# Attention followed by a feed-forward block on one core: another set of ranks for a scheduler that orders the program

## The chip, the cores and the metric

The kernel runs on 1 of the 8 cores of one Trainium2 chip. A core has five engines with a queue of instructions each: TensorE (PE; weight loads are shown as PEld), VectorE (DVE), ScalarE (ACT), GpSimd (POOL) and SyncE (SP), which here only issues DMAs. The metric is the device time of one execution in microseconds (us).

## The reference

Attention over 32 heads (4 batches of 8; 1152 keys, head dimension 64), with queries averaged in pairs (576 rows), then a feed-forward block with a leaky ReLU whose slope is given per feature.

```python
q_pool = q.reshape(B, H, S // 2, 2, D).mean(axis=3)
scores = (1 / sqrt(D)) * q_pool @ k.T
scores = scores - scores.max(axis=-1)
attn = exp(scores); attn = attn / (attn.sum(axis=-1) + 1e-9)
x = (attn @ v).transpose(0, 2, 1, 3).reshape(B * S // 2, H * D)   # 2304 x 512
h = x @ w_in                                                      # 512 -> 2048
g = maximum(h, 0) + alpha * minimum(h, 0)
return g @ w_out                                                  # 2304 x 512
```

## The kernel before

Every fp32 operand is split in a rounded part and a rest (two tiles), so that products run as fp32r matmuls. The work of head n:

- **Preparation** (`head_prep`). Heads 0 to 3 load their own queries (L674, the first head L770); from head 4 on a pair of heads shares a tile `qs`: the even queries are loaded (L662, SP, 576 KB), and the odd ones are added on the way in by a DMA that accumulates (L667, issued by POOL, 576 KB). Keys `kk` come with L684 (576 KB). ACT rounds q and k (L689, L694), DVE makes the rests (L722 for q, L709 for k; `LD` and `TD` say for which heads on DVE, else POOL). Two DMAs within SBUF, the key halves, put halves of the rounded keys into tile `k3` (L649, 2 x 144 KB, named `k<-k`). `qs` and `kk` have two buffers each.
- **Maxima** (`head_max`). PE forms rounded scores (L894) and DVE takes the row maxima from PSUM (L910), six times a head; a seventh, smaller one (PE L875, DVE L884), reads the key halves. The maxima are transposed (PE L928, ACT L932, DVE L937) and a small DMA (L944, 2.5 KB, `q<-mm`) writes them as the last row of the operand `q2`, so that the score matmul subtracts them. This runs two heads ahead of the scores.
- **Scores and weighted sum** (`head_main`). For each of 9 chunks of 128 keys and each half of the queries two matmuls (L966, then L967, which reads `q2`), an exp on ACT (L979) into one of the `pa` slots, adds of `pa` tiles for the denominators (L992, on DVE for the chunks named in `ADDS`, else on POOL), and the product with v (L1007; v comes with L818).
- **End of a pair** (`pair_end`). Sums over the keys (PE L1029), then a chain of small DMAs through DRAM (`rsd` L1044, `rc` L1045, reciprocal on DVE L1047, `rrd` L1050, broadcasts `r` L1059), the normalisation on DVE and ACT (L1066, L1073, L1078) and four stores `xs<-x` (L1088, 144 KB each).

The feed-forward block (`hidden`, `low_sweep`, `high_sweep`, all its matmuls on L471) needs the outputs of 8 heads and of weights that ACT and DVE convert (`w_convert`, loads L395). In the beginning PE multiplies a constant tile (`warm`, L1137) between the first maxima.

**What sets the order.** Nothing here runs in the order of the Python code. `Scheduler` keeps a list of ready tasks for each engine with a guessed duration, and places again and again the task that can start first; among tasks of an engine that could start within a slack (`SLP`, `SLA`, `SLD`) the lowest rank `prio` wins:

```python
for s, t in cand:
    if s <= at + self.slack[eng]:
        p = t.prio + (self.col_cost if eng == PE and t.col != self.col else 0.0)
        if key is None or p < key:
            key, pick, first = p, t, s
```

The order in which tasks are placed is the order in which each engine's queue holds them on the chip; an engine waits at each instruction until its operands are there, and all behind it wait too. SP is such a queue: a store that waits for DVE holds back the loads behind it. Ranks are numbers like `n - Q0` (load of `qs`) or `n - KR` (rounding). `SWITCH` is the head after which the placement hands PSUM banks to the feed-forward block, `PB` and `AB` are numbers of `pa` slots for exps and for added tiles.

Of the kernel before, what the change touches and what calls it, by code (L numbers as in the profile page):

```python
# [219 lines left out]
def attention_ffn(  # L220
# [7 lines left out]
    q0: bass.AP,  # L228
    out: bass.AP,
    NLO: int = 5,  # L230
    PB: int = 14,
    QB: int = 2,
    DF: int = 1713,
    D0: int = 1171.677,
    AQ: int = 0,
    F0: float = 1.51,
    F2: float = 2.12,
    FD: tuple = (1, 1, 0),
    WE: float = 11.307,
    WG: int = 1,  # L240
    WT: float = 6.848,
    WM: int = 1,
    WB: int = 300,
    WN: int = 4,
    TO_PE: int = 164,
    FROM_PE: int = 6,
    SLP: int = 37,
    SLA: int = 171,
    SLD: int = 40,
    QL: float = -0.025,  # L250
    KL: float = 1.864,
    KR: float = 1.387,
    KS: float = -0.601,
    M0: float = 1.047,
    E0: float = 0.482,
    BD: int = 4,
    SD: tuple = (2, 16),
    LD: tuple = (0, 33),
    TD: tuple = (0, 33),
    SR: float = 0.47,  # L260
    Q0: float = -1.805,
    Q1: float = 4.468,
    GROUPS: tuple = ((3, 8), (8,)),
    PARTS: tuple = (((0, 1, 2), (3, 4), (5, 6), (7, 8)), ((0, 1, 2, 3), (4, 5, 6, 7, 8))),
    JH: int = 8,
    AB: int = 8,
    ADDS: tuple = ((2, 7, 8), (2, 7, 8)),
    PL: int = 2,
    LV: int = -9,
    LW: int = -9,  # L270
    GSB: int = 1,
    YSB: int = 4,
    R0: float = 6.415,
    R1: float = -3.03,
    R2: float = 3.013,
    R3: float = -1.183,
    W0: float = 4.578,
    W1: float = 3.204,
    W2: float = 24.069,
    W3: float = -2.969,  # L280
    YL: float = 0.328,
    MS: float = 0.123,
    EARLY: tuple = ((0, 1, 2), (3, 5), ()),
    LATE: tuple = ((0, 1, 2), (3, 5), (0, 1, 2, 3, 5)),
    SWITCH: int = 11,
    GL: float = 11.249,
    COL: float = 0.256,
    HW: float = -0.368,
    XB: int = 4,
    PT: int = 17,  # L290
    VB: int = 2,
# [4 lines left out]
    QA: float = 1.0,  # L296
    REUSE: int = 6,
    NW: tuple = (464, 460, 460, 460, 460),
    RP: float = 32.195,
    RS: float = 0.808,  # L300
    RM: int = 31,
    RATE: float = 385.825,
):
    nc = tc.nc
    NH, D, S = kt.shape[0], kt.shape[1] // 2, kt.shape[2]
# [940 lines left out]
```

## Time and profile before

| | |
|---|---|
| time, median of 3 runs | 872.32 us (871.31 to 877.17) |
| the profiled execution | 870.35 us |
| its span, first to last instruction | 868.6 us |
| PE busy | 842.8 us, 97% |
| DVE / ACT / POOL busy | 584.4 / 498.1 / 194.3 us |
| mean granted TensorE clock | 0.997 |

Attention takes the first 476 us of the span, the rest is feed-forward alone. A busy PE is not PE at its peak, since matmuls overlap in the records; idle time of PE is the surer sign.

### The profile page before, as it was taken

What the parts mean: (1) busy time and instruction counts of PE and PEld (TensorE: products, weight loads), DVE (VectorE), ACT (ScalarE), POOL (GpSimd) and SP (SyncE); (2) the same over time, 40 slices, a digit from 0 to 9 for tenths busy, and PEclk for the clock granted to TensorE, in tenths of its full rate; (3) what the DMA queues carried; (4) which work ended last, traced back from release to release, by engine and by line L of the source; (5) the groups of instructions that cost most, each with busy time, mean ns of one, the idle gap of its engine ahead of it and who ended that gap; (6) DMA issues with size and microseconds to landing.
All of it is one profiled execution on the core that took longest, in us unless ns stands there. A gap on an engine that the chain in (4) does not pass through costs nothing.

```text
span 868.6 us, 15141 instructions
## 1 busy us (share of the span) xinstructions
PE 842.8 (97%) x5461; PEld 713.4 (82%) x5461; DVE 584.4 (67%) x901; ACT 498.1 (57%) x1233; POOL 194.3 (22%) x149
## 2 busy tenths in 40 slices
PE   9999998999999999999999999999999999999997
PEld 7677676777777777777887999998888898988986
DVE  6898998999999988888987499932232232332322
ACT  4667787777787777867774576743223233232321
POOL 4333334445344453453541000000000000000000
PEclk9999999999999999999999999999999999999999
DMA  8637656786667556574343577647230331200301
GB/s 294 172 89 206 182 169 184 189 233 183 157 190 217 157 182 158 160 206 108 95 134 120 158 265 239 217 127 208 68 102 5 88 88 42 69 20 1 88 0 44
DMA packets 76081, 121.90 MB, mean 140 GB/s; under 512 B 21771, under 2 KB 46950, under 8 KB 76006
## 3 DMA queue, kind: packets, MB, share of 16 engines
q1 hardware_dynamic: 73990, 112.67, 42.9%
q0 software_dynamic: 2016, 8.26, 5.6%
q8 instruction: 43, 0.70, 0.3%
q14 instruction: 32, 0.26, 0.1%
HBM read 92.65 MB, written 19.02 MB: 129 GB/s over the span
## 4 chain that ended last, share of the span: by engine, by line
PE 75%; DVE 9%; DMA 8%; ACT 4%; issue 2%; SPq 0%; POOL 0%; DVEq 0%; ACTq 0%; POOLq 0%
PE bank L471 41%; PE bank L1007 13%; PE bank L966 6%; PE bank L967 5%; PE bank L894 5%; DMA k<-k 5%; PE bank L1029 2%; DVE bx L910 2%; DMA wraw<-wt 2%; ACT pa L979 2%; PE bank L875 1%; DVE pa L992 1%; DMA qs<-qt 1%; PE bank L1137 1%; DVE wbits L413 1%
## 5 line engine op out<-in xcount | busy, mean ns | idle before, releaser
L992 POOL TENSOR_TENSOR pa<-pa,pa 128x576 f32<-128x576 f32 x120 | 174.7, 1464 | 245.4 <-ACT pa L979 199.4
L979 ACT ACTIVATE pa<-bank 128x288 f32<-128x288 f32 x576 | 202.5, 407 | 29.1 <-PE bank L967 22.7
L910 DVE TENSOR_REDUCE bx<-bank 128x2 f32<-128x768 f32 x194 | 176.4, 944 | 15.7 <-PE bank L894 14.8
L966 PE MATMUL bank<-q,k 128*128 128x288 f32 x576 | 170.6, 311 | 1.3 <-ACT pa L979 1.2
L967 PE MATMUL bank<-q,k 65*128 65x288 f32 x576 | 165.1, 298 | 0.2 <-ACT q L852 0.2
L1007 PE MATMUL bank<-pa,vv 128*64 128x288 f32 x1152 | 148.5, 410 | 0.0
L1007 PEld LDWEIGHTS bank<-pa,vv 128*64 128x64 f32 x1152 | 79.1, 137 | 55.7 <-issue 6.6
L966 PEld LDWEIGHTS bank<-q,k 128*128 128x128 f32 x576 | 109.2, 190 | 10.2 <-ACT pa L979 3.8
L516 DVE TENSOR_TENSOR gw<-gs,gw 128x460 fp32r<-128x460 f32 (+1 forms) x55 | 35.1, 639 | 120.0 <-ACT gw L511 119.8
L967 PEld LDWEIGHTS bank<-q,k 65*128 65x128 f32 x576 | 109.8, 191 | 0.4 <-ACT q L852 0.4
L511 ACT ACTIVATE gw<-gs 128x460 fp32r<-128x460 f32 (+1 forms) x55 | 32.4, 589 | 125.2 <-PE bank L471 115.2
L894 PE MATMUL bank<-k,q 128*128 128x384 f32 x372 | 97.9, 345 | 3.7 <-DVE bx L910 3.4
L471 PE MATMUL bank<-wlow,wh 128*128 128x460 f32 (+1 forms) x320 | 92.9, 371 | 0.0
L471 PE MATMUL bank<-gw,wh 128*128 128x460 f32 (+1 forms) x320 | 92.8, 371 | 0.0
L505 DVE SCALAR_TENSOR_TENSOR gs<-gs,nal 128x460 f32<-128x460 f32 (+1 forms) x55 | 38.4, 699 | 52.3 <-ACT gs L500 52.3
L992 DVE TENSOR_TENSOR pa<-pa,pa 128x576 f32<-128x576 f32 x88 | 67.0, 762 | 2.3 <-POOL pa L992 2.0
L471 PE MATMUL bank<-gs,wlow 128*128 128x288 f32 x480 | 66.3, 296 | 1.3 <-ACT neg L500 1.1
L471 PE MATMUL bank<-x,wlow 128*128 128x288 f32 x480 | 67.4, 295 | 0.0
L894 PEld LDWEIGHTS bank<-k,q 128*128 128x128 f32 x372 | 60.5, 192 | 7.5 <-DVE bx L910 5.2
L471 PEld LDWEIGHTS bank<-gs,wlow 128*128 128x128 f32 x480 | 64.1, 188 | 2.5 <-ACT neg L500 1.3
L471 PEld LDWEIGHTS bank<-wlow,wh 128*128 128x128 f32 x320 | 60.1, 188 | 7.0
L471 PEld LDWEIGHTS bank<-gw,wh 128*128 128x128 f32 x320 | 60.1, 188 | 6.8
(99 smaller groups left out, 1123.4 us busy)
## 6 DMA issues: line engine op xcount, KB each, us to landing
kk<-kt SPq DMA_DIRECT2D x31, 576.0 KB
wraw<-wt SPq DMA_DIRECT2D x32, 512.0 KB
qs<-qt SPq DMA_DIRECT2D x18, 576.0 KB
vv<-vt SPq DMA_DIRECT2D x32, 288.0 KB
xs<-x SPq DMA_DIRECT2D x64, 144.0 KB
x<-xs SPq DMA_DIRECT2D x32, 288.0 KB
k<-k SPq DMA_DIRECT2D x62, 144.0 KB
qs<-qt POOLq DMA_DIRECT2D x14, 576.0 KB, 6.0
```

The costliest lines, as they stand in the source:

```text
L471: nc.tensor.matmul(out=ps[:, :n], lhsT=w[a, c // DMO][:, c % DMO:c % DMO + P], rhs=lo(hl), start=(first and i == 0), stop=(last and i == 2),)
L505: lambda: nc.vector.scalar_tensor_tensor(out=flat(pos), in0=flat(neg), scalar=nal[:, f:f + 1], in1=flat(pos), op0=ALU.mult, op1=ALU.add),
L511: ACT, act(n), lambda: nc.scalar.activation(out=gs.t[:, 0, :n], in_=flat(pos), func=AF.Copy),
L516: lambda: nc.vector.tensor_tensor(out=gs.t[:, 1, :n], in0=flat(pos), in1=gs.t[:, 0, :n].bitcast(F32), op=ALU.subtract),
L894: nc.tensor.matmul(out=ms.t[:, i, :JW], lhsT=(flat_of(raw, F32R) if raw else q1.t)[:, c:c + P], rhs=k1.t[:, j * JW:(j + 1) * JW], start=Tr ...
L910: lambda c=c, e=e, step=step, m=len(pair), ms=ms: nc.vector.tensor_reduce(out=bx.t.rearrange("p t j -> p (t j)")[:, c:e + 1:step], in_=ms. ...
L966: nc.tensor.matmul(out=ps.t[:, :HQ], lhsT=k1.t[:, s], rhs=q1.t[:, q], start=True, stop=False)
L967: nc.tensor.matmul(out=ps.t[:, :HQ], lhsT=k2[n % 2][:, s], rhs=q2[n % 2][:, PAD + q.start:PAD + q.stop], start=False, stop=True)
L979: lambda ps=ps, p=p, h=h: nc.scalar.activation(out=p.t[:, h], in_=ps.t[:, :HQ], func=AF.Exp, scale=SCALE),
L992: lambda a=a, b=p, part=part, e=e: e.tensor_tensor(out=part.t, in0=a.t, in1=b.t, op=ALU.add),
L1007: nc.tensor.matmul(out=av.t[h * D:(h + 1) * D, :HQ], lhsT=vv.t[:, e], rhs=p.t[:, h], start=(e == 0), stop=(e == NC - 1),)
L1029: nc.tensor.matmul(out=ps.t[g * 32:(g + 1) * 32, :HQ], lhsT=ones, rhs=acc[n + g // 2][j].t[:, g % 2], start=j == 0, stop=j == m - 1, tile_ ...
```

## The change

Only the default numbers of `attention_ffn` change, 40 of them; no code. Most are ranks, guessed durations and slacks. Those that can be read by themselves, and two of the ranks:

```diff
-    PB: int = 14,
+    PB: int = 13,
-    FD: tuple = (1, 1, 0),
+    FD: tuple = (0, 0, 0),
-    WM: int = 1,
+    WM: int = 2,
-    TD: tuple = (0, 33),
-    SR: float = 0.47,
-    Q0: float = -1.805,
-    Q1: float = 4.468,
+    TD: tuple = (3, 33),
+    SR: float = -0.087,
+    Q0: float = -2.673,
+    Q1: float = 4.659,
-    AB: int = 8,
-    ADDS: tuple = ((2, 7, 8), (2, 7, 8)),
+    AB: int = 10,
+    ADDS: tuple = ((3, 6), (2, 7, 8)),
...
-    SWITCH: int = 11,
+    SWITCH: int = 12,
```

`FD` moves the first head's query add (L781) and query rest (L796) from POOL to DVE; `TD` moves the key rests (L709) of heads 1 and 2 from DVE to POOL; `ADDS` moves 8 adds (L992), one in each of heads 0 to 7, from DVE to POOL. PE has the same matmuls but for L1137: 14 of 512 columns and 53 of 128 become 17 of 512 and 28 of 256. Elsewhere the counts are the same and the order is another one. From head 12 on PE's own order changes in about nine places, by a step or two, until the feed-forward matmuls begin among the scores of head 30; they begin there in both kernels.

**SP, one pair of heads** (from the key halves of head 27 to those of head 28; `k_...<-k_...` are key halves, `q_0_108<-mm` is the row of maxima). Before:

```order
L1050 DMA rrd<-rc 128x9
L649 DMA k_4045<-k_4042 64x576 x2
L684 DMA kk<-kt 128x1152
L1059 DMA r<-rrd 64x288 x4
L944 DMA q_0_108<-mm 1x5x128
L818 DMA vv<-vt 128x576
L662 DMA qs<-qt 128x1152
L1088 DMA xs_75<-x_4177 64x576 x2
L1088 DMA xs_75<-x_4179 64x576 x2
L818 DMA vv<-vt 128x576
L649 DMA k_4205<-k_4182 64x576 x2
```

With the change:

```order
L1050 DMA rrd<-rc 128x9
L662 DMA qs<-qt 128x1152
L649 DMA k_4027<-k_4020 64x576 x2
L1059 DMA r<-rrd 64x288 x3
L944 DMA q_0_108<-mm 1x5x128
L1059 DMA r<-rrd 64x288
L818 DMA vv<-vt 128x576
L684 DMA kk<-kt 128x1152
L1088 DMA xs_75<-x_4154 64x576 x2
L1088 DMA xs_75<-x_4157 64x576 x2
L818 DMA vv<-vt 128x576
L649 DMA k_4183<-k_4159 64x576 x2
```

The load `qs` has moved from behind the row of maxima to ahead of head 27's key halves; the load `kk` that stood behind those halves now stands behind the row of maxima, ahead of the four stores `xs`; one broadcast `r` has slipped behind the row. The stores and `vv` ahead of head 28's halves stay.

**POOL, the adds of head 25 and the accumulating load of the last pair** (head 25 has four adds on POOL, for chunks 1, 3, 5 and 6). Before:

```order
L992 TENSOR_TENSOR pa_97<-pa_100,pa_101 128x576
L992 TENSOR_TENSOR pa_97<-pa_97,pa_89 128x576
L992 TENSOR_TENSOR pa_102<-pa_90,pa_91 128x576
L992 TENSOR_TENSOR pa_102<-pa_102,pa_92 128x576
L667 DMA qs<-qt 128x1152
L992 TENSOR_TENSOR pa_103<-pa_95,pa_96 128x576
```

With the change:

```order
L992 TENSOR_TENSOR pa_103<-pa_103,pa_92 128x576
L992 TENSOR_TENSOR pa_95<-pa_99,pa_100 128x576
L667 DMA qs<-qt 128x1152
L992 TENSOR_TENSOR pa_95<-pa_95,pa_88 128x576
L992 TENSOR_TENSOR pa_101<-pa_89,pa_90 128x576
L992 TENSOR_TENSOR pa_101<-pa_101,pa_91 128x576
```

In the first piece L667 stands behind all four adds of head 25, in the second behind the first of them. It is so for each pair p from the ninth on (against the adds of head 2p - 5). Of the earlier ones pairs 4, 6, 7 and 8 are moved up by one to three adds, pairs 2, 3 and 5 go back by one or two.

**DVE, from the maxima of head 1 to those of head 2** (`mx_111` is of head 1, `mx_110` of heads 0 and 2, L722 are query rests, L680 the query adds of heads 2 and 3). Before:

```order
L992 TENSOR_TENSOR pa_97<-pa_97,pa_90 128x576
L680 TENSOR_TENSOR qs<-qs 128x576 x2
L910 TENSOR_REDUCE bx<-bank_117 128x2
L884 TENSOR_REDUCE mx_110<-bank_118 128x1
L922 TENSOR_REDUCE mx_111<-bx 128x4
L722 TENSOR_TENSOR q_382<-qs,q_382 64x576
L937 TENSOR_REDUCE mm<-bank_121 1x64
L992 TENSOR_TENSOR pa_100<-pa_95,pa_96 128x576
L722 TENSOR_TENSOR q_421<-qs,q_421 64x576
L709 TENSOR_TENSOR k_0_106<-kk,k_320 64x1152
L910 TENSOR_REDUCE bx<-bank_117 128x2
```

With the change:

```order
L910 TENSOR_REDUCE bx<-bank_117 128x2
L680 TENSOR_TENSOR qs<-qs 128x576
L922 TENSOR_REDUCE mx_111<-bx 128x4
L992 TENSOR_TENSOR pa_98<-pa_93,pa_94 128x576
L680 TENSOR_TENSOR qs<-qs 128x576
L722 TENSOR_TENSOR q_366<-qs,q_366 64x576
L937 TENSOR_REDUCE mm<-bank_120 1x64
L884 TENSOR_REDUCE mx_110<-bank_118 128x1
L910 TENSOR_REDUCE bx<-bank_117 128x2
L910 TENSOR_REDUCE bx<-bank_118 128x2
```

In the second piece one add (L992), one query rest and the key rest (L709) between the last maxima of head 1 and the first of head 2 are gone or stand further down. Further up (not shown) the key rest of head 1 has gone from DVE as well, and on PE the first two maxima matmuls of head 1 stand ahead of the second score of head 0 instead of behind the fourth.

## Rows read from the trace of the kernel before

**Rows 1.** The page's first part: busy time, share of the span, instructions.

```profile
PE 842.8 (97%) x5461; PEld 713.4 (82%) x5461; DVE 584.4 (67%) x901; ACT 498.1 (57%) x1233; POOL 194.3 (22%) x149
```

**Rows 2.** Windows: us, busy of each engine (instructions), granted clock, DMA share, GB/s.

```profile
16.50:50.00 33.50, 30.28 (x179) 23.33 (x178) 29.39 (x39) 22.95 (x61) 10.39 (x8) 0.95 0.63 171
50.00:162.00 112.00, 107.29 (x808) 81.12 (x807) 99.82 (x148) 84.22 (x219) 39.30 (x29) 1.00 0.62 173
162.00:430.00 268.00, 258.59 (x1900) 202.51 (x1899) 241.69 (x355) 205.00 (x538) 121.25 (x90) 1.00 0.63 173
476.40:868.60 392.20, 386.16 (x2150) 356.49 (x2142) 163.61 (x284) 151.29 (x330) 0.00 (x0) 1.00 0.34 102
```

**Rows 3.** Waits of PE, whole span: us in total, times, longest.

```profile
PE bank L875 <- DMA k<-k: 10.4, 8, 2.7
PE bank L894 <- DVE bx L910: 3.4, 4, 1.7
PE bank L875 <- DVE bx L910: 1.7, 3, 0.6
```

**Rows 4.** SP's queue, heads 26 to 30: start us, issuing time, line.

```profile
374.66 0.47 SPq L662 DMA_DIRECT2D qs<-qt  x1
380.84 3.17 SPq L1088 DMA_DIRECT2D xs<-x  x4
...
384.74 1.12 SPq L649 DMA_DIRECT2D k<-k  x2
...
410.91 1.12 SPq L649 DMA_DIRECT2D k<-k  x2
```

**Rows 5.** PE, maxima on key halves, heads 28 and 30: start, duration, [idle].

```profile
389.94 0.50 PE L875 MATMUL bank<-k,bd 128*128 128x288 f32 x2 [1.23 <-DMA k<-k]
...
415.49 0.42 PE L875 MATMUL bank<-k,bd 128*128 128x288 f32 x2
```

**Rows 6.** POOL, the accumulating load of the last pair.

```profile
379.20 0.88 POOL L667 DMA_DIRECT2D qs<-qt  x1 [0.42 <-issue]
```

**Rows 7.** DMA queues in 380.5:384 (all there is): packets, MB, share.

```profile
q0 software_dynamic: 122, 0.56, 95.4%
```

**Rows 8.** DMA queues in 408.5:414 (all there is).

```profile
q1 hardware_dynamic: 629, 1.18, 80.8%
```

**Rows 9.** SP's queue, heads 20 and 21.

```profile
286.45 0.33 SPq L1050 DMA_DIRECT2D rrd<-rc  x1
288.61 1.15 SPq L649 DMA_DIRECT2D k<-k  x2
...
293.53 0.75 SPq L944 DMA_DIRECT2D q<-mm  x1
```

**Rows 10.** PE: key halves of head 21, then the row of maxima of head 20.

```profile
295.04 0.42 PE L875 MATMUL bank<-k,bd 128*128 128x288 f32 x2
...
297.28 0.29 PE L967 MATMUL bank<-q,k 65*128 65x288 f32 x1
```

**Rows 11.** DVE, heads 1 and 2.

```profile
17.18 1.35 DVE L709 TENSOR_TENSOR k<-kk,k 64x1152 fp32r<-64x1152 f32 x1
...
26.26 0.76 DVE L992 TENSOR_TENSOR pa<-pa,pa 128x576 f32<-128x576 f32 x1
...
29.99 1.37 DVE L722 TENSOR_TENSOR q<-qs,q 64x576 fp32r<-64x576 f32 x1
...
32.49 0.76 DVE L722 TENSOR_TENSOR q<-qs,q 64x576 fp32r<-64x576 f32 x1
33.27 1.35 DVE L709 TENSOR_TENSOR k<-kk,k 64x1152 fp32r<-64x1152 f32 x1
```

**Rows 12.** PE, first maxima of head 2, first score of head 1.

```profile
35.55 0.61 PE L894 MATMUL bank<-k,q 128*128 128x384 f32 x2 [1.67 <-DVE bx L910]
36.00 0.30 PE L966 MATMUL bank<-q,k 128*128 128x288 f32 x1
```

**Rows 13.** Window just after, columns as in Rows 2.

```profile
36.66:40.08 3.42, 3.42 (x14) 3.42 (x14) 2.48 (x3) 1.70 (x5) 0.38 (x1) 0.50 0.95 268
```

**Rows 14.** POOL, an add of head 0.

```profile
29.32 1.42 POOL L992 TENSOR_TENSOR pa<-pa,pa 128x576 f32<-128x576 f32 x1 [3.54 <-ACT pa L979]
```

## What the change should do: the prediction

> **What bounds the kernel now.** The page's first part comes first: PE is busy for 97% of the span, and no other engine for more than 67% [rows 1]. So time is won where PE stands idle, or where its clock is low, and nowhere else. The second view is a table of windows by stage [rows 2]; in each row the reader subtracts PE's busy time from the length. From 476.4 us on, feed-forward alone, 6.0 of 392.2 us are idle. In attention it is 3.2 us between 16.5 and 50 (where the mean granted clock is 0.95 and not 1), 4.7 between 50 and 162, 9.4 between 162 and 430: 17.3 us in all. The third view says what those idle times wait for [rows 3]. The largest item is L875, the small seventh maximum, which waits 10.4 us in 8 waits for the key halves, longest 2.7. Waits of PE for DVE's row maxima come next: 3.4 + 1.7 = 5.1 us. These two are what other ranks can win.
>
> Why are the key halves late? In SP's queue the halves of head 28 are issued at 384.74, right behind four stores that were issued from 380.84 on [rows 4]; PE wants them 1.23 us before it gets them at 389.94 [rows 5]. So 5.20 us passed from issue to use, and PE would have used them 3.97 after the issue. The view of the DMA queues tells what was ahead: POOL issues the accumulating load at 379.20 [rows 6], and in the 3.5 us from 380.5 to 384 the only packets are that queue's, 0.56 MB, with the engines 95% busy [rows 7]. The stores, issued at 380.84, move nothing in that time. Head 30 is the control: there is no accumulating load left, SP's order is the same, all traffic of the stretch is on SP's queue [rows 8], and L875 starts at 415.49 with no idle time, 4.58 us after its issue at 410.91 [rows 4, 5]. That is an upper bound on the delivery, since PE did not wait.
>
> [...]
>
> **The accumulating load.** The change puts L667 ahead of three adds of head 2p - 5 that stood before it, for the pairs from the ninth on, and two to three adds earlier for pairs 4 and 6 to 8. The adds come at roughly one in two chunks, so the load is issued some 6 us earlier: about 373 instead of 379 for the last pair. Its 3.5 us of traffic then end near 378, before the stores are issued at 380.8. Then the even heads' halves meet what head 30's met, and the wait is gone: 10.4 us is the bound. One stall of 8 can survive where other loads (`vv`, weights) stand in front, so I take **8 us** off; the ends are 10.4 and 0 (if the DMA engines are as full without it).
>
> **What the load meets at its new place.** The load `qs` now stands ahead of the odd head's halves, `kk` behind the row of maxima. The halves of head 21 are issued at 288.61 and used, without waiting, at 295.04 [rows 9, 10]: 6.43 us. The queue is free to issue `qs` from 286.45 on, some 1.8 us ahead of the halves. The stretch without an accumulating load moved 1.18 MB in 5.5 us with the engines 81% busy [rows 8], 215 GB/s, or 265 with full engines; `qs`, 0.59 MB, takes 2.2 to 2.7 us by that. So at most 0.9 us are left in front, and 4.58 + 0.9 = 5.5 is under 6.43: nothing, with 0.95 us in hand. The row of maxima (L944) is tighter. For head 20 it is issued at 293.53 and first read at 297.28 [rows 9, 10], 3.75 us, and the accumulating load now falls about there, behind that row by an estimated 1 us. I charge **2.5 us** over all pairs. The ends are 0 and 15, half of the price of the slower rival below.
>
> **The start.** Between the maxima of head 1 and of head 2 DVE loses two key rests to POOL (2 x 1.35), an add to POOL (0.76), and one query rest that moves behind (0.76) [rows 11]: 4.2 us ahead of the point where PE waits 1.67 us for DVE at 35.55 and the first score of head 1 starts at 36.00 [rows 12]. [...] DVE's relief alone would give 4.2. I take **4 us**, with ends 0.5 (the query chain over ACT is next, or the key rests on POOL come late) and 4.9. POOL's own price for a key rest has no row; its adds take 1.42 against DVE's 0.76 [rows 14, 11], so a rest of 1.35 would take about 2.5, an estimate, and PE must not need it for that long.
>
> Moving the first head's query add and rest to DVE is costed at nothing: PE multiplies constant tiles there, waiting for the first maxima. [...]
>
> **Heads 2 to 10.** One add fewer on DVE in each of heads 0 to 7 takes 6 us off DVE in a stage where PE waits for it little by little. **1 us** off, between 0 and 2.
>
> **The feed-forward part.** PE's order is the same but for small steps, and `SWITCH` moves nothing there, since the feed-forward matmuls begin among head 30's scores in both. Nothing, ±1.
>
> **Sum.** -8 + 2.5 - 4 - 1 = -10.5 us against the profiled execution's 870.35 gives 859.9. That execution lies 2.0 below the median 872.32, so the time is 861.8.
>
> **The rivals.**
> - *Larger gain.* All idle time of attention goes and the clock holds: 17.3 + 1.7 = 19.0, or 853.3. For it: with the accumulating load out of the way the whole chain of the pair comes earlier. Against: some of those waits are on ACT and on DVE's order, which the change does not touch. Between 11 and 19 us of gain lie 853 to 859.
> - *Nothing to be seen.* The stall moves from the halves of the even heads to those of the odd ones: the DMA engines are busy for 0.62 of the time in attention anyway [rows 2], and the load's 3.5 us have to stand in front of something. Each of 13 odd heads would need to wait about 0.8 us to return 10.4. Time 872, ±3.
> - *POOL holds up DVE.* An add on POOL ran from 29.32 to 30.74 [rows 14], and the query rest that DVE started beside it at 29.99 took 1.37 instead of 0.76 [rows 11]: 0.6 us for one meeting. Eight more adds on POOL, each with a meeting, cost 4.9 us and most of the start's gain: 861.8 + 4.9 = 866.7.
> - *Slower: the row of maxima behind the accumulating load.* If L667 goes out just before the row L944 is issued, the row (2.5 KB) waits out up to 3.5 us of traffic [rows 7], and all scores of that head wait with it. The nine pairs 7 to 15 would pay 31.5 us; after the gains of 8, 4 and 1 that is +18.5 on the median, or 891. It breaks even at 13 / 9 = 1.4 us a pair. For it: the load moves to exactly this place, the margin is 3.75 us minus what delivery needs. Against: the order of SP has one broadcast fewer ahead of the row, so it goes out earlier.
>
> [...]
>
> **How the numbers follow.** A measurement of this kernel tells about 1% from no change, 8.7 us: below 863.6 is faster, above 881.0 slower. The forecast (859 to 867 around 861.8) has 0.50, of which 0.33 lies below 863.6; the larger gain 0.15; nothing to be seen 0.14; POOL against DVE 0.08; slower 0.13, of which 0.12 lies above 881. Faster: 0.33 + 0.15 = 0.48. Slower: 0.12. The rest, 0.40, is within 1%. The range is to leave out 2 in 10: 852 takes in the larger gain but for its end, and 874 most of the case without effect; left out are the slower rival and a few hundredths on either side.
>
> **What would show it.** If the first step is right, PE's waits of L875 for `k<-k` fall from 10.4 to under 3 us, the accumulating queue's packets no longer overlap the issue of the four stores, and L875 of head 28 has no idle time. If the second is right, the first score of head 1 starts near 32 instead of 36.00, with a granted clock of 1 behind it. New idle time at L967 behind `q<-mm`, or at L875 in odd heads, would be the slower or the empty case; DVE rows of L722 or L992 well over 0.76 in heads 0 to 7 the fourth. The prediction is wrong if the idle time of PE between 50 and 430 us does not fall below 8 us.

## The result, and the profile after

The changed kernel takes 861.82 us (median of 4 runs, 861.03 to 866.28) against 872.88 for the kernel before (4 runs, one more than in the table ahead of the prediction); the ratio is 0.9876, with a 95% interval of 0.9827 to 0.9925, so it is 1.2% faster. The profiled execution took 861.74 us with a span of 859.9, 8.7 less than before.

The page's first part and the windows of the same stretches as [rows 1, 2], with one more row for a stretch of low clock:

```profile
PE 841.0 (98%) x5439; PEld 711.5 (83%) x5439; DVE 580.3 (67%) x893; ACT 501.0 (58%) x1233; POOL 207.4 (24%) x157
```

```profile
16.50:50.00 33.50, 30.45 (x193) 23.87 (x195) 27.95 (x40) 23.99 (x60) 16.26 (x11) 0.95 0.68 168
50.00:162.00 112.00, 110.63 (x853) 84.14 (x850) 100.57 (x146) 85.31 (x225) 48.92 (x36) 1.00 0.66 182
162.00:430.00 268.00, 262.79 (x1918) 206.59 (x1917) 245.22 (x362) 205.45 (x541) 123.02 (x89) 0.99 0.65 174
...
44.98:48.60 3.62, 3.62 (x17) 3.07 (x17) 3.31 (x6) 3.41 (x9) 1.41 (x1) 0.53 0.72 140
```

PE's idle time between 50 and 430 us went from 14.1 to 6.6 us, under the 8 that the prediction named. Between 16.5 and 50 it did not go: 3.1 instead of 3.2 us, with the same mean clock. The waits of PE, as in [rows 3], say what is left:

```profile
PE bank L966 <- ACT pa L979: 2.9, 2, 2.6
PE bank L966 <- DVE mm L937: 2.7, 1, 2.7
PE bank L875 <- DMA k<-k: 1.3, 3, 0.5
```

The wait for key halves fell from 10.4 to 1.3 us, and two waits of 2.6 and 2.7 us at L966, the first of the two matmuls of a score, are new. The first stands among the scores of head 1 and waits for an exp, the second among those of head 12 and waits for L937 of head 13, which has to free a PSUM bank. Where they stand, and the key halves of heads 28 and 30 as in [rows 5], shows PE's timeline:

```profile
32.20 0.29 PE L966 MATMUL bank<-q,k 128*128 128x288 f32 x1
...
43.86 0.40 PE L966 MATMUL bank<-q,k 128*128 128x288 f32 x1 [2.63 <-ACT pa L979]
...
193.50 0.40 PE L966 MATMUL bank<-q,k 128*128 128x288 f32 x1 [2.72 <-DVE mm L937]
...
380.38 0.51 PE L875 MATMUL bank<-k,bd 128*128 128x288 f32 x2 [0.50 <-DMA k<-k]
...
406.16 0.43 PE L875 MATMUL bank<-k,bd 128*128 128x288 f32 x2
```

The first score of head 1 starts at 32.20 instead of 36.00 [rows 12]. For the last pair, SP's queue and POOL (compare [rows 4, 6]):

```profile
359.26 0.33 SPq L662 DMA_DIRECT2D qs<-qt  x1
...
372.03 3.34 SPq L1088 DMA_DIRECT2D xs<-x  x4
...
376.10 1.11 SPq L649 DMA_DIRECT2D k<-k  x2
```

```profile
364.44 0.87 POOL L667 DMA_DIRECT2D qs<-qt  x1
```

The accumulating load is now issued 7.6 us ahead of the four stores (before: 1.6), and 15.9 us ahead of L875 of head 28 (before: 10.7). It landed 7.3 us after its issue, ahead of the stores, and between 372 and 374.5 us, but for one fetch of instructions, only SP's queue has packets:

```profile
q1 hardware_dynamic: 153, 0.41, 52.6%
```

So the sign that the prediction named, no overlap of that load with the stores, is there; its other sign, no idle time ahead of L875 of head 28, is not quite (0.50 us).

Where the time came from is best read at fixed places of the work: the start of each head's first exp (L979) in the two traces.

| first exp of head | before | after | difference | since the row above |
|---|---|---|---|---|
| 1 | 36.47 | 32.72 | -3.75 | -3.75 |
| 2 | 50.38 | 47.09 | -3.29 | +0.46 |
| 8 | 135.35 | 131.12 | -4.23 | -0.94 |
| 11 | 177.90 | 170.02 | -7.88 | -3.65 |
| 13 | 204.95 | 201.13 | -3.82 | +4.06 |
| 18 | 270.87 | 266.73 | -4.14 | -0.32 |
| 27 | 393.16 | 383.60 | -9.56 | -5.42 |
| 31 | 444.05 | 435.64 | -8.41 | +1.15 |
| end of the span | 868.6 | 859.9 | -8.7 | -0.3 |

The key halves give 9.1 us (heads 8 to 11 and 18 to 27), the beginning 3.3, and heads 11 to 13 take back 4.1, where the second new wait stands. Of these 4.1 us 2.3 are more idle time of PE, and 1.7 come from half a clock for 3.4 us behind the wait (there L966 and L967 follow each other every 0.24 us, in the same place of the kernel before every 0.13), which the kernel before does not have there:

```profile
195.20:198.61 3.41, 3.41 (x16) 3.41 (x15) 2.73 (x4) 2.31 (x6) 2.63 (x2) 0.50 0.54 174
```

Heads 27 to 31 take back another 1.2 with PE idle for 0.2 us at most; 9 more PE instructions stand there, 5 of them of the feed-forward part. What makes this dearer was not tried.

### The profile page after: what moved, and what is told of

Its sections match the earlier page's. It is cut to its first block, busy times and chain, and to the rows that moved or that the text cites. A ratio compares the mean times of both kernels' runs of the same rounds, so it can differ in the third digit from the quotient of the medians.

```text
span 859.9 us, 15160 instructions
## 1 busy us (share of the span) xinstructions
PE 841.0 (98%) x5439; PEld 711.5 (83%) x5439; DVE 580.3 (67%) x893; ACT 501.0 (58%) x1233; POOL 207.4 (24%) x157
## 4 chain that ended last, share of the span: by engine, by line
PE 75%; DVE 10%; DMA 7%; ACT 3%; issue 2%; SPq 2%; POOL 0%; DVEq 0%; ACTq 0%
PE bank L471 41%; PE bank L1007 12%; PE bank L966 7%; PE bank L967 6%; PE bank L894 5%; DMA r<-rrd 2%; PE bank L1029 2%; DMA qs<-qt 2%; ACT pa L979 1%; DVE bx L910 1%; DMA wraw<-wt 1%; PE bank L875 1%; DMA k<-k 1%; DVE pos L505 1%; DVE k L709 1%
## 5 line engine op out<-in xcount | busy, mean ns | idle before, releaser
L992 POOL TENSOR_TENSOR pa<-pa,pa 128x576 f32<-128x576 f32 x128 | 186.6, 1484 | 227.0 <-ACT pa L979 200.4
L979 ACT ACTIVATE pa<-bank 128x288 f32<-128x288 f32 x576 | 203.1, 410 | 24.5 <-PE bank L967 17.6
L966 PE MATMUL bank<-q,k 128*128 128x288 f32 x576 | 171.5, 312 | 6.4 <-ACT pa L979 2.9
L967 PE MATMUL bank<-q,k 65*128 65x288 f32 x576 | 166.1, 300 | 0.4 <-ACT q L852 0.4
L966 PEld LDWEIGHTS bank<-q,k 128*128 128x128 f32 x576 | 109.7, 191 | 14.8 <-ACT pa L979 7.4
L967 PEld LDWEIGHTS bank<-q,k 65*128 65x128 f32 x576 | 110.4, 192 | 0.6 <-ACT q L852 0.6
L495 ACT ACTIVATE gs<-bank 128x460 f32<-128x460 f32 (+1 forms) x55 | 30.6, 556 | 110.2 <-PE bank L471 109.5
L471 PEld LDWEIGHTS bank<-x,wlow 128*128 128x128 f32 x480 | 64.8, 188 | 0.9 <-ACT neg L500 0.5
```

What stands on the lines that cost most here:

```text
L471: nc.tensor.matmul(out=ps[:, :n], lhsT=w[a, c // DMO][:, c % DMO:c % DMO + P], rhs=lo(hl), start=(first and i == 0), stop=(last and i == 2),)
L495: ACT, act(n, True), lambda: nc.scalar.activation(out=flat(pos), in_=ps.t[:, :n], func=AF.Relu),
L966: nc.tensor.matmul(out=ps.t[:, :HQ], lhsT=k1.t[:, s], rhs=q1.t[:, q], start=True, stop=False)
L967: nc.tensor.matmul(out=ps.t[:, :HQ], lhsT=k2[n % 2][:, s], rhs=q2[n % 2][:, PAD + q.start:PAD + q.stop], start=False, stop=True)
L979: lambda ps=ps, p=p, h=h: nc.scalar.activation(out=p.t[:, h], in_=ps.t[:, :HQ], func=AF.Exp, scale=SCALE),
L992: lambda a=a, b=p, part=part, e=e: e.tensor_tensor(out=part.t, in0=a.t, in1=b.t, op=ALU.add),
```

## The experiments

Each is compared with the kernel before on its own chip (medians there 874.0 us for runs 1 to 4, 874.1 for 5 to 8, 873.5 for 9 to 12), as a ratio with its 95% interval. "First exp" is that of head 1, 36.47 before and 32.72 after.

**1. KR alone.** `KR` ranks ACT's rounding and its copies L640, and DVE's query rests.

```diff
-    KR: float = 1.387,
+    KR: float = 1.573,
```

> The kernel before with one of the 40 numbers changed, the rank of rounding KR (1.387 to 1.573). By the order of the instructions this alone moves the accumulating load of pairs 7 to 15 ahead of three adds and the load qs ahead of the odd head's key halves, while PE keeps its order up to head 12. My theory (the accumulating load is the cause of the late key halves): PE's waits of L875 for k<-k fall from 10.4 to under 3 us, head 1's first score stays at 36, and the time falls by 5 to 8 us, to 865 to 868. Rival (the gain is from the beginning, the stall only moves to other heads): 870 to 874, with the waits of L875 or new ones at L966 or L967 near 10 us in sum.

Measured: 866.28 us, ratio 0.9922 (0.9888 to 0.9956), 6.8 us by the ratio; first exp 36.77. Waits of PE, the first two lines (none is left at L875 for `k<-k`):

```profile
PE bank L966 <- DVE mm L937: 4.0, 3, 2.3
PE bank L894 <- DVE bx L910: 2.7, 3, 1.7
```

One rank of forty takes the stall away. Less than its 10.4 us is gained: two of the waits at L966, near 197 and 265 us, take 3.9 us, and behind each the clock is halved for 3.4 us (the mean from 162 to 430 us is 0.99, in the kernel before 1.00 [rows 2]). `KR` also brings the new wait at L966 in head 12, so that this wait belongs to the same move.

**2. The changed kernel without KR.**

```diff
-    KR: float = 1.573,
+    KR: float = 1.387,
```

> The changed kernel with KR back at 1.387, so that the accumulating load of most pairs from 7 on stands where it stood before (pairs 10 and 11 keep an earlier place), and the beginning stays changed up to head 6. My theory: the waits for k<-k come back to some 6 to 9 us and the time rises by 4 to 7 us, to 866 to 869. Rival (the gain is from the beginning): 861 to 863.

Measured: 873.53 us, ratio 1.0016 (0.9980 to 1.0052): nothing is left of the gain, more than I expected, though the first exp stays at 33.03. Waits of PE:

```profile
PE bank L875 <- DMA k<-k: 9.4, 7, 2.1
PE bank L966 <- ACT pa L979: 5.4, 3, 3.5
```

The stall is back, and the wait of 2.6 us near 43.9 has become 3.5. Two waits of 1.6 and 1.5 us, at 243 and 282, have no match in the changed kernel, so the key halves are not the whole loss. The other 39 numbers give nothing that can be told without it.

**3. The numbers of the beginning alone.**

```diff
-    FD: tuple = (1, 1, 0),
+    FD: tuple = (0, 0, 0),
-    TD: tuple = (0, 33),
+    TD: tuple = (3, 33),
-    ADDS: tuple = ((2, 7, 8), (2, 7, 8)),
+    ADDS: tuple = ((3, 6), (2, 7, 8)),
...
```

> The kernel before with the numbers of the beginning alone (FD, F0, F2, TD, ADDS and the three of the constant-tile multiplications) as in the changed one. The accumulating load of the later pairs keeps its old place in most pairs, so this is the start term by itself with the disturbance that it makes in the middle. My theory: head 1's first score starts some 3 to 4 us earlier, the waits for k<-k stay at 8 us or more, and the time is 867 to 870. Rival (the beginning is the whole gain): 860 to 864.

Measured: 886.51 us, ratio 1.0152 (1.0106 to 1.0197). The first exp is at 32.16, as expected, but the waits for `k<-k` sum to 4.7 us and not to the 8 or more that I expected, and the time is off too: between the first exps of heads 19 and 23 this kernel loses 11.4 us more. One window of it:

```profile
332.00:336.00 4.00, 1.91 (x7) 1.83 (x8) 3.77 (x5) 2.23 (x6) 2.15 (x2) 0.75 0.98 220
336.00:340.00 4.00, 4.00 (x17) 4.00 (x16) 1.76 (x3) 2.89 (x7) 1.82 (x2) 0.50 0.42 82
```

PE stands idle for 2.1 us of the first row and has a granted clock of 0.50 in the second. In this order feed-forward matmuls stand among the scores from 289 us on (in the changed kernel from 428), so part of the 11.4 us is work done earlier. As a measure of the beginning alone this run is inconclusive; the 4.3 us gained at head 1 were worth nothing here, with another order behind it.

**4. The changed kernel with the old beginning** (the reverse of 3).

> The changed kernel with the numbers of the beginning back at the old ones; the accumulating load of pairs 7 to 15 keeps its new place. My theory: the start term is lost and nothing else, so 864 to 867, with waits for k<-k under 3 us. Rival (the beginning is the whole gain): 870 to 874. A second rival, that eight more adds on POOL hold DVE up and cost most of what the beginning gives: 860 to 863.

Measured: 863.61 us, ratio 0.9888 (0.9846 to 0.9930), against 0.9876 for the change: the same within the interval. `k<-k` waits 0.6 us. And the first exp is at 33.53, 2.9 us earlier than before without `FD`, `TD` and `ADDS`. So these three are not what started head 1 earlier, or at most by the last 0.8 us.

**5. The kernel before, with an eighth of the accumulated bytes.**

```diff
-nc.gpsimd.dma_start(out=qs.t, in_=qt[n // 2, 1], accum_op=ALU.add)
+nc.gpsimd.dma_start(out=qs.t[:, :, :72], in_=qt[n // 2, 1, :, :, :72], accum_op=ALU.add)
```

> The kernel before, order unchanged on every engine; the accumulating load moves 72 of 576 columns, an eighth of its bytes (so the odd queries are added in for those columns alone). My theory (the 3.5 us of its traffic hold up the stores and key halves behind them): waits for k<-k fall from 10.4 to under 2 us with the load still in its old place, and the time falls by 6 to 10 us against the kernel before. Rival (the place in the queues matters, not the bytes: the halves are late because the four stores stand ahead of them): the waits stay above 7 us and the time within 3 us.

Measured: 860.30 us, ratio 0.9859 (0.9806 to 0.9912). Of PE's waits for `k<-k` one remains:

```profile
PE bank L875 <- DMA k<-k: 1.4, 1, 1.4
```

Same order on every engine, fewer bytes, and the stall is gone but for one wait of 1.4 us, whose cause is open: the traffic of L667 was the cause of the rest. The gain, 9.0 us in span, is that of the 9.0 us of waiting.

**6. The changed kernel with the same cut.**

> The changed kernel, order unchanged, the accumulating load again an eighth of its bytes (odd queries added in for 72 of 576 columns). It asks what the load still costs at its new place. My theory: PE's two long waits in the changed kernel, 2.6 us near 43.9 (exps behind a copy that waits for the pair's queries) and 2.7 us near 193.5 (DVE late because the broadcasts r stand behind the load), both fall under 1 us, as does the half clock after the first; 4 to 8 us faster than the changed kernel, 14 to 19 below the kernel before. Rival (these waits come from the order of ACT and DVE, weights among exps): within 2 us of the changed kernel, 9 to 13 below the kernel before.

Measured: 855.54 us, ratio 0.9827 (0.9763 to 0.9891). PE's longest wait, and what is left for key halves, are now

```profile
PE bank L894 <- DVE mx L884: 1.4, 1, 1.4
...
PE bank L875 <- DMA k<-k: 0.3, 1, 0.3
```

Both waits at L966, near 43.9 and 193.5, are gone, and the clock is 1.00 from 16.5 to 50 us. At its new place the load still costs 4 us by the two ratios and 7 by the spans of the profiled executions (859.9 and 852.8).

**7. The transfer numbers alone.**

```diff
-    DF: int = 1713,
-    D0: int = 1171.677,
+    DF: int = 1729,
+    D0: int = 1100.92,
-    RATE: float = 385.825,
+    RATE: float = 384.919,
```

> The kernel before with the three guessed transfer numbers alone (RATE, DF, D0) as in the changed one. In the order, the accumulating load of the later pairs keeps its old place, and at the beginning DVE's transposed maximum of head 1 stands ahead of head 2's query rests, although FD, TD and ADDS are the old ones. My theory after the run with the old beginning: these numbers, not the work moved to POOL, make head 1's first exp earlier, by 2.5 to 3.5 us (33 to 34 instead of 36.5); waits for k<-k stay at 8 to 11 us, and the time is 0 to 4 us below the kernel before. Rival (it takes FD, TD and ADDS): head 1's first exp stays at 36 to 37, time within 1 us.

Measured: 871.51 us, ratio 0.9978 (0.9944 to 1.0011), no change that can be told; first exp 33.69. DVE's timeline and PE's waits:

```profile
29.72 0.27 DVE L937 TENSOR_REDUCE mm<-bank 1x64 fp32r<-1x128 f32 x1
```

```profile
PE bank L875 <- DMA k<-k: 9.4, 8, 2.1
```

In the kernel before, L937 of head 1 stood behind a query rest of 1.37 us [rows 11], after which its row could be written. These three numbers move it ahead, and that gives 2.8 us at the first exp of head 1 and 5.0 at that of head 8. By the end of this execution nothing is left, though the waits for key halves are a little shorter than before. What takes the gain is the clock: around four of these waits it is halved, for 17.1 us in all, which costs half of that, some 8.5 (means of 0.98 from 50 to 162 us and 0.97 from 162 to 430), while the profiled execution of the kernel before has no half clock there (1.00 in both [rows 2]). The longest such stretch:

```profile
362.87:369.70 6.83, 6.40 (x24) 5.67 (x26) 4.06 (x7) 4.50 (x12) 1.44 (x2) 0.50 0.21 72
```

The ten executions have mean clocks of 0.988 (the profiled one) to 0.996, so this loss differs from one to the next.

**8. Head 2's key rest back on DVE.**

```diff
-    TD: tuple = (3, 33),
+    TD: tuple = (2, 33),
```

> The changed kernel with the key rest of head 2 back on DVE (TD from 3 to 2); PE and ACT keep their order. POOL is then free 2.6 us earlier, and the accumulating load of the first shared pair goes out near 30.5 instead of 32.8. My theory: the 2.6 us wait near 43.9 and the stretch of half clock behind it shrink by 2 us or more; 1 to 4 us faster than the changed kernel, 12 to 15 below the kernel before. Rival (the pair's queries are held by the transfers issued in between, key halves, v and keys, or DVE's 1.35 us more delay the maxima): no change or 1 us slower than the changed kernel.

Measured: 857.11 us, ratio 0.9824 (0.9770 to 0.9877). The load of the first shared pair, the copy on ACT that waits for it, and the window:

```profile
31.93 1.01 POOL L667 DMA_DIRECT2D qs<-qt  x1 [1.59 <-DMA qs<-qt]
```

```profile
38.83 0.52 ACT L640 ACTIVATE bd<-qs 64x64 fp32r<-64x64 f32 x2 [1.02 <-DMA qs<-qt]
```

```profile
16.50:50.00 33.50, 32.99 (x238) 25.26 (x239) 31.00 (x45) 25.60 (x65) 13.20 (x10) 1.00 0.71 184
```

In the changed kernel the same copy ran at 42.85 after 5.15 us of waiting, and all exps on ACT stood behind it. The load goes out only 0.8 us earlier (31.93, not the 30.5 that I had worked out, since it must wait for the even queries), yet the copy starts 4 us earlier. The likely reason, not tried by itself: SP now issues the keys of head 4 behind the key halves, at 33.09 and not at 30.93, so they no longer stand ahead of it in the DMA engines. PE's wait and the half clock behind it are gone (1.00 in the window, 0.95 in the changed kernel).

**9. Pair 8's load behind the broadcasts.** On the kernel of 8:

```diff
-                    writes=[pair_qs[0]], deps=[load], prio=n - Q1, ...
+                    writes=[pair_qs[0]], deps=[load] + (r_loads[4] if n == 16 else []), prio=n - Q1, ...
...
+                r_loads.setdefault(n // 2, []).append(t)
```

> The previous kernel (changed, with head 2's key rest on DVE) with one dependence more: the accumulating load of pair 8 waits for the four broadcasts r of the pair two before it in the queue, which were issued beside it. By the order it goes out behind all adds of head 11 instead of behind the first; all other pairs stay. My theory (DVE waits for the broadcasts because this load shares the DMA engines with them, and PE's 2.7 us wait in head 14 follows from that): DVE's wait at L1066 near 180 falls from 2.2 to under 0.5 us, PE's 2.7 us wait at L966 to under 1, and the time falls by 1 to 3 us below the kernel without it. Rival (that wait comes from the weight conversion on ACT and DVE, which stand in front of the exps): the wait stays, time unchanged within 1 us. A second rival: the load now stands ahead of head 14's key halves, as in the kernel before, and PE waits 1 to 2 us for them instead.

Measured: 853.87 us, ratio 0.9766 (0.9708 to 0.9824): the fastest kernel here, 2.3% below the one before. POOL, DVE (line numbers behind the edit are one higher: L1067 is L1066), and all that PE waits for key halves:

```profile
177.68 0.87 POOL L667 DMA_DIRECT2D qs<-qt  x1
```

```profile
177.69 0.82 DVE L1067 TENSOR_TENSOR r<-avs,r 128x288 f32<-128x288 f32 x2
```

```profile
PE bank L875 <- DMA k<-k: 1.2, 3, 0.7
```

DVE no longer waits for this `r`, and PE's 2.7 us wait is gone (it stood among the scores of head 12, not in head 14 as I wrote above). Heads 11 to 13 take 26.7 us here, 30.2 in run 8 and 27.0 in the kernel before: 3.5 us gained on run 8, more than I expected. Besides the load, one instruction each on DVE, ACT and SP changes its place by a step or two. The weights on ACT and DVE stand in the same place as before, so they only passed the delay on. The third case, a wait for head 14's halves, costs 0.4 us.

**10. The changed kernel again**, unaltered, on the chip of 9, 11 and 12.

> The changed kernel unaltered, on the same chip as the three beside it, so that differences of 3 to 5 us can be told. Both theories: 0.985 to 0.990 of the kernel before, with the 2.6 us wait near 43.9 and the half clock behind it again.

Measured: 862.10 us, ratio 0.9860 (0.9800 to 0.9921), with waits of 2.4 and 2.7 us at L966. The half clock that I expected behind the first of them did not come:

```profile
43.70:47.20 3.50, 3.50 (x23) 2.98 (x25) 2.60 (x4) 3.40 (x11) 1.22 (x2) 1.00 0.75 111
```

So the same wait of the same program is followed by half a clock in one execution (2.63 us, then 0.53 for 3.62 us) and not in another (2.4 us, then 1.00). Run 9 is 8.2 us faster than the change on the same chip.

**11. Both early key rests on DVE** (TD from 3 to 1).

> The changed kernel with both early key rests (heads 1 and 2) back on DVE (TD from 3 to 1), which undoes the change to TD; PE, ACT and SP keep their order of the kernel with TD 2. It asks whether taking key rests off DVE brings anything. My theory by now: what counts is POOL being free for the accumulating load, so this is as fast as with TD at 2, 4 us faster than the changed kernel, within 1.5 us. Rival (the relief of DVE that my prediction counted on, 1.35 us a rest): head 1's first exp 1 us or more later than 33.0, and the time 1 to 2 us above that with TD at 2.

Measured: 858.54 us, ratio 0.9828 (0.9764 to 0.9892), first exp 32.73: not to be told from 8, and head 1 starts as in the changed kernel. Taking key rests off DVE brought nothing.

**12. FD back**, on the kernel of 8.

```diff
-    FD: tuple = (0, 0, 0),
+    FD: tuple = (1, 1, 0),
```

> The changed kernel with head 2's key rest on DVE (TD 2) and FD back at its old value, so that the first head's query add and rest run on POOL again. My prediction costed this part at nothing; in the changed kernel the last maxima of head 0 come 1.0 us earlier than before. My theory now: worth about 1 us at the first score of head 0 (16.5 instead of 15.5), some of it lost later: 0 to 2 us slower than the kernel with TD 2 alone. Rival (PE waits with constant tiles in any case): the same within 0.5 us at head 1's first exp.

Measured: 864.74 us, ratio 0.9890 (0.9831 to 0.9948), some 6 us slower than 8; the first exp of head 1 is at 37.21, 4.3 us later, though that of head 0 is 2.5 earlier (16.16 against 18.63). DVE stands idle ahead of the maxima of head 1, and PE has half its clock for 10.2 us, part of it ahead of the first exp:

```profile
20.20 1.82 DVE L910 TENSOR_REDUCE bx<-bank 128x2 f32<-128x768 f32 x2 [3.09 <-PE bank L894]
```

```profile
34.49:44.73 10.24, 9.92 (x39) 8.21 (x39) 7.06 (x10) 6.41 (x19) 4.22 (x3) 0.50 0.39 73
```

I expected 0 to 2 us. FD sets the order of all of head 1, not only the first head's preparation. Which of its moves costs the 4.3 us was not tried. Another 6.8 us of half clock stand at 194.9, where run 8 has 3.4; at half of their length the two stretches cost 6.8 us more than in run 8, of 9.9 between the two spans.

## Why the prediction was right

**The accumulating load** (-8): right, in mechanism and size. The waits fell by 9.1 us, the ledger of heads 8 to 11 and 18 to 27 holds 9.1, and the load went out as far ahead as forecast. Run 5 shows the cause without any change of order, runs 1 and 2 that one rank decides it. Why `KR` does so is argued from the code, not shown: rounding and query rests are what frees a buffer of `qs`.

One reading under it was too generous. The prediction counts 3.5 us in which the stores moved nothing; but beside no load the stores issued at 407.78 had their first packet 1.1 us later, so those issued at 380.84 could have had theirs at 382 and were held up to 384.05, some 2 us.

**What the load meets** (+2.5): sized too small, and wrong in place. Nothing waits for the row of maxima; the broadcasts `r` came late instead. DVE's timeline in the changed kernel:

```profile
185.69 0.46 DVE L1066 TENSOR_TENSOR r<-avs,r 128x288 f32<-128x288 f32 x1 [2.69 <-DMA r<-rrd]
```

The load was issued at 177.16, the broadcasts from 177.01 on. One pair of nine pays 4.1 us; run 9, which moves that load, gives 3.5 back. The prediction looked at the row alone because PE waits for it directly; the way over DVE was not priced, nor the half clock behind the wait.

**The start** (-4): the size was nearly right, 3.3 us, the step was not. The prediction put it down to work taken off DVE by `TD` and `ADDS`, counted FD as nothing, and expected a granted clock of 1 behind the first score. Run 11 shows that the key rests gave nothing, runs 4 and 7 that 2.8 to 2.9 us of it come without FD, TD and ADDS, from the transfer numbers among others: DVE's order (L937 ahead of a query rest) and not its load. In both runs some 50 more PE instructions than before stand between the first exps of heads 1 and 2, so head 1 alone flatters them; at head 8 they are 3.5 and 5.0 us ahead, the change 4.2. The half clock was not returned: it moved from 36.66 (0.50 for 3.42 us [rows 13]) to 44.98 (0.53 for 3.62), behind the new wait at 43.86, and a second stretch came behind the wait at 193.50 (0.50 for 3.41). The 1.7 us in the larger gain and in the end of 4.9 us (3.2 of idle time and 1.7) are an estimate, half of those 3.42 us; the change did not bring them, but run 8 has 1.00 from 16.5 to 50 us. The wait at 43.86 goes when run 8 gives head 2's key rest back to DVE, so moving that rest cost time, where the prediction counts it as 1.35 us of relief. Run 12 shows that FD is worth some 6 us when its neighbours are as in run 8, much of it by the clock, so the parts of the start don't add.

**Heads 2 to 10** (-1) and **feed-forward** (0): -0.9 (heads 2 to 8) and -0.3, beside the 1.2 us that heads 27 to 31 lost.

**The rivals.** *Slower*: its mechanism exists, at another wait and for one pair. *Nothing to be seen*: refuted; no odd head waits for its halves. *POOL holds up DVE*: refuted as a cost. Rows of L722 stretch here too, but seldom:

```profile
29.97 1.55 DVE L722 TENSOR_TENSOR q<-qs,q 64x576 fp32r<-64x576 f32 x1
```

Up to 150 us, what DVE's adds and query rests took beyond 0.76 us and its key rests beyond 1.35 sums to 1.3 us, and to 1.9 in the kernel before. *Larger gain*: not by this change; it is there with one more number and one dependence (run 9, 853.9; the rival said 853.3).

The time itself, 861.8, owes something to chance. Against the profiled execution the sum was 1.9 us too good (859.9, measured 861.74): the key halves gave 1.1 us more than taken, the start 0.7 less, the collision in heads 11 to 13 took 1.6 more, and heads 27 to 31, to which no term was given, took 1.2. The 2.0 us added from the profiled execution to the median made up for it; the changed kernel's median lies only 0.1 above its profiled execution.

## What to carry to other kernels

When a small transfer is late, look at what has the DMA engines before it, on any queue; shrink that transfer's bytes with the order held, and see whether the wait goes (in run 5 9.0 of 10.4 us went). Here the load that was moved out of the way of the key halves (9.1 us) landed in that of the broadcasts (4.1 us back): price every transfer issued within its length, those for engines off the critical path too. In a program whose order comes from ranks, undo ranks one by one and read the order of each: here one of forty carried most of the gain, and two other parts taken alone were worth nothing or less than nothing. Look at the clock in every trace that you compare: in the changed kernel the wait of 2.72 us at 193.50 cost another 1.7 us by the half clock behind it, and the wait of 2.4 us in run 10 had a clock of 1.00 behind it.

## What the runs showed of the hardware

In three stretches two queues did not share the DMA engines evenly; in two of the three the one that came first held them. (q0 is POOL's queue, q1 SP's.) In the kernel before, stores issued at 380.84 moved nothing until 384, beside POOL's load with 122 packets and 0.56 MB [rows 4, 7]; beside no load, those issued at 407.78 had packets within 1.2 us. The other way round, the changed kernel's first load, issued at 32.76 behind keys, `v` and key halves on SP's queue, moved nothing from 34 to 36 us; its first packet came 3.9 us after its issue, that of the last pair's load 1.7 us after. The DMA queues of that stretch (packets count whole where they start, so a share can pass 100%):

```profile
q1 hardware_dynamic: 236, 0.50, 101.3%
```

But in 180 to 183 us of that kernel both moved, POOL's load ahead:

```profile
q0 software_dynamic: 89, 0.40, 71.0%
q1 hardware_dynamic: 82, 0.08, 12.5%
```

There the two are nearly equal in packets, 89 against 82, and not in bytes.
